# Moving a quarter of one reduction from TensorE to VectorE, and the value masks from VectorE to ScalarE, in a cached-attention decode kernel

## The chip, the cores and the metric

One core of one Trainium2 chip. The metric is the device time of one execution in microseconds (us); lower is better. Several runs are taken and the median is given. One further execution is profiled: its trace gives every instruction's start and duration on each engine, TensorE (PE, with its weight loads as PEld), VectorE (DVE), ScalarE (ACT), GpSimd (POOL) and SyncE (SP, which here only issues DMAs), the semaphores that ended waits, and the DMA packets.

## What is computed

A decode step for 4 batch entries of one token each, model width 512. An adaLN-conditioned attention block with a K and V cache (32 heads of 128, 4096 cached keys), and behind it a gated MLP with a spatial gate:

```python
mod = (_silu(c) @ w_mod).reshape(c.shape[0], 6, 1, -1)
sa, ca, ga, sb, cb, gb = (mod[:, 0], mod[:, 1], mod[:, 2], mod[:, 3], mod[:, 4], mod[:, 5])
h = _layernorm(x) * (1 + ca) + sa
q = (h @ wq).reshape(B, 1, 32, 128).transpose(0, 2, 1, 3)
scores = einsum('bhqd,bhkd->bhqk', q, k_cache) * 128 ** -0.5
o = einsum('bhqk,bhkd->bhqd', softmax(scores), v_cache)
x = x + ga * (o.transpose(0, 2, 1, 3).reshape(B, 1, 4096) @ wo)
h = _layernorm(x) * (1 + cb) + sb
x = x + gb * mixer(h)        # gelu(h @ w_in), halves z1 and layernorm(z2), z1 * (w_sp z2 + b_sp) @ w_out
```

K and V are bf16, 134 MB each. Each cached number is used once.

## The kernel before

**Tiles.** The work on K and V is cut into 32 tiles. Tile i is one batch entry (i mod 4) and one group of four heads (i div 4, eight groups). Its K is 4.19 MB and lies in SBUF as `kt`: 128 partitions by 128 key slots (`NJ`) by 128 numbers (`DH`), partitions 0 to 31 holding the keys of the first head of the group, 32 to 63 those of the second, and so on. V lies the same way as `vt`. There are two buffers for K and two for V.

**Scores of a tile.** With one query there is nothing for TensorE to reuse, so VectorE multiplies K with the query, copied to every partition (`qbc`), in place and in two halves of 64 slots (`mult`, L291). The product then has to be summed over its 128 numbers for each slot. `reduce_d` (L299) does part of that on TensorE: matmuls with the identity add slices of the product in PSUM, 512 columns at a time, 16 matmuls for 64 slots; what is left, 8 partial sums a slot, VectorE adds from PSUM (`sum8`, L318). In tiles 1 to 29, only half of the second 64 slots goes this way (`on_pe` gives 32; 8 matmuls, 16 partial sums a slot), and VectorE sums the other 32 slots straight from SBUF (`sum_rest`, L311).

**Softmax.** `scores` takes the row maximum (L327), spreads it over the 32 partitions of its head by a copy, a 32x32 transpose and a maximum (L329, L331, L333), scales it by -1/sqrt(128) (L334) and has ScalarE take the exponentials head by head into `pbd` (L341), with the row sums `rs`. `norm_r` (L352) puts `rs` into its head's column of `rsb` with a mask; one matmul and a reciprocal (`norm_a`, `norm_b`) give the normaliser for four tiles at once.

**Values.** `pv` (L381) multiplies probabilities with V in 32 matmuls into a PSUM bank (`opss`, two of them); four sets of rows and four column blocks come out, of which each row set has one useful block. `o_pick` (L389, L393) picks them on VectorE with masks `selg`: one product and three multiply-adds of 128x128 f32. `o_cols` (L401) sums the rows that belong together and turns the result with one f32 matmul against `sel4`; `o_scale` (L420, L423) copies it out and normalises it.

**Order.** The order of instructions is written out by hand (a manual schedule), and each engine runs its own in that order. In iteration i: first half product of tile i, softmax of tile i-1, value pick of tile i-3, TensorE sums of the first half, second product, `norm_r` of i-1, `o_scale` of i-3, partial sums of the first half, TensorE sums of the second half, `sum_rest`, then the request for K of tile i+2, which needs the buffer of tile i and so waits for `sum_rest`, then `pv` of i-2 and the request for V of tile i, which waits for `pv` of i-2. All large loads are issued by SP, in this order, on one queue. At iterations 11, 19, 27 and 31 `dealt` regroups finished heads, and `project` multiplies them with `wo`.

**The ends.** Before the first K tile come `wq` and most of `w_mod` (6.8 MB). In iteration 2 the four parts of `wo` and its last rows are loaded; behind the last V come the MLP's weights. Tile 31's V is loaded in five pieces, and the last group of heads (tiles 28 to 31) is handled on its own. Then follow the second layer norm, the MLP and one store.

Of the kernel before, what the change touches and what calls it, by code (L numbers as in the profile page):

```python
# [9 lines left out]
F32 = mybir.dt.float32  # L10
AF = mybir.ActivationFunctionType
ALU = mybir.AluOpType
AX = mybir.AxisListType
PSUM = bass.MemoryType.PSUM

HQ = 4
KC = 64
# [10 lines left out]
def kernel(  # L28
# [16 lines left out]
    nc = tc.nc  # L45
    P = 128
    B, _, D = A_x.shape
    _, H, SK, DH = A_k_cache.shape
# [9 lines left out]
    G = 4  # L58
# [17 lines left out]
    def ps_sm(shape, dtype=F32):  # L76
        return psum.tile(shape, dtype, name="sm", bufs=3)
# [210 lines left out]
    def mult(i, kc):  # L288
        kt = kts[i][:, kc * KC:(kc + 1) * KC, :]
        g, b = divmod(i, B)  # L290
        nc.vector.tensor_tensor(out=kt, in0=kt, in1=bc(qbc[:, g, b, :], KC), op=ALU.mult)  # L291

    def reduce_d(i, kc):
        ns = on_pe(i, kc)
        rd = 512 // ns
        kt = kts[i][:, kc * KC:kc * KC + ns, :]
        red = ps_red().rearrange("p (n r) -> p n r", r=rd)
        for m in range(DH // rd):
            nc.tensor.matmul(  # L299
                red, lhsT=ident_bf, rhs=kt[:, :, m * rd:(m + 1) * rd],  # L300
                start=(m == 0), stop=(m == DH // rd - 1),
            )
        st[i, "red", kc] = red

    def on_pe(i, kc):
        return KC // 2 if kc == 1 and 1 <= i < L - 1 else KC

    def sum_rest(i):
        n0 = KC + on_pe(i, 1)
# [13 lines left out]
    def scores(i):  # L323
        sum8(i, 1)
        S = st.pop((i, "S"))
        mrow = wk.tile([P, 1], F32, name="mrow")
        nc.vector.tensor_reduce(out=mrow, in_=S, axis=AX.X, op=ALU.max)  # L327
        mb = wk.tile([P, R], F32, name="mb")
        nc.vector.tensor_copy(out=mb, in_=mrow.to_broadcast([P, R]))  # L329
        mt = wk.tile([P, R], F32, name="mt")  # L330
        nc.vector.transpose(mt, mb)  # L331
        nM = wk.tile([P, 1], F32, name="nM")
        nc.vector.tensor_reduce(out=nM, in_=mt, axis=AX.X, op=ALU.max)  # L333
        nc.vector.tensor_scalar(  # L334
            out=nM, in0=nM, scalar1=-att_scale, scalar2=None, op0=ALU.mult
        )
        pbd = pbds[i % 3]
        rs = wk.tile([P, 1], F32, name="rs", bufs=3)
        for q in range(HQ):
            r = slice(R * q, R * (q + 1))  # L340
            nc.scalar.activation(  # L341
                out=pbd[r, :, q], in_=S[r, :], func=AF.Exp, bias=nM[r, :],
                scale=att_scale, accum_out=rs[r, :],
            )
        st[i, "rs"] = rs

    def norm_r(i):

        g, b = divmod(i, B)
        if b == 0 or g == NQ - 1:  # L350
            st[g, "rsb"] = wk.tile([P, B, HQ], F32, name="rsb", bufs=2)
        nc.vector.tensor_scalar(  # L352
            out=st[g, "rsb"][:, b, :], in0=mask4, scalar1=st.pop((i, "rs")), scalar2=None, op0=ALU.mult
        )
# [21 lines left out]
    def pv(i):  # L376

        for m in range(NJ // G):
# [4 lines left out]
                start=(m < 4), stop=(m >= NJ // G - 4), tile_position=(0, g),  # L383
            )

    def o_pick(i):
        ops = opss[i % 2]
        osb = wk.tile([P, DH], F32, name="osb")
        nc.vector.tensor_scalar(  # L389
            out=osb, in0=ops[:, 0, :], scalar1=selg[:, 0:1], scalar2=None, op0=ALU.mult  # L390
        )
        for g in range(1, G):
            nc.vector.scalar_tensor_tensor(  # L393
                out=osb, in0=ops[:, g, :], scalar=selg[:, g:g + 1], in1=osb,
                op0=ALU.mult, op1=ALU.add,
            )
        st[i, "osb"] = osb

    def o_cols(i):
        op = ps_sm([P, HQ])  # L400
        nc.tensor.matmul(op, lhsT=st.pop((i, "osb")), rhs=sel4, start=True, stop=True)  # L401
        st[i, "op"] = op
# [9 lines left out]

    def o_scale(i):
        g, b = divmod(i, B)
        op = st.pop((i, "op"))[:, None, :]
        bs = whole(i)
        if g < NQ - 1:
            if b == 0:
                st[g, "o"] = wk.tile([P, B, HQ], F32, name="oU", bufs=2)
            nc.vector.tensor_copy(out=st[g, "o"][:, b:b + 1, :], in_=op)  # L420
            op = st[g, "o"]
        if bs:
            nc.vector.tensor_tensor(  # L423
                out=oTs[:, g * B + bs.start:g * B + bs.stop], in0=op, in1=st.pop((i, "rz")), op=ALU.mult
            )
# [44 lines left out]
    def dealt():  # L470
        if "pp" in st:
            pp, k = st.pop("pp")
            n = SETS[k]
            own = wk.tile([P, n * B, n], F32, name=f"own{n}", bufs=1)
            nc.vector.tensor_tensor(
                out=own, in0=pp.rearrange("p r b h -> p (r b) h"),
                in1=bc(mask8 if n == 2 * HQ else mask4, n * B), op=ALU.mult,
            )
            od = wk.tile([P, n, B], BF16, name="od", bufs=1)
            with nc.allow_low_precision("all but one term of each sum are zero"):  # L480
                nc.vector.tensor_reduce(
                    out=od.rearrange("p r b -> p (r b)"), in_=own, axis=AX.X, op=ALU.add
                )
            st["od"] = od, k
# [60 lines left out]
    for i in range(NT):  # L545
        more = list(QPLAN.get(i, ()))
        mult(i, 0)
        if i >= 1:
            scores(i - 1)
        if i >= 2:  # L550
            norm_b(i - 2)
        add_up()
        rows_up()
        dealt()
        if i >= 3:
            o_pick(i - 3)
        reduce_d(i, 0)
        if i >= 3:
            o_cols(i - 3)
        if more:  # L560
            queries(more.pop(0))
        mult(i, 1)
        if i >= 1:
            norm_r(i - 1)
        if i >= 3:
            o_scale(i - 3)
        sum8(i, 0)
        reduce_d(i, 1)
        sum_rest(i)
        load_k(i + 2)  # L570
        if i >= 1:
            norm_a(i - 1)
        project()
        if i - 3 in ends:
            deal(ends[i - 3])
        while more:
            queries(more.pop(0))
        if i >= 2:
            pv(i - 2)
        if i == 0:  # L580
            load_v(1)
        elif 2 <= i < L:
            load_v(i)
        if i == 2:
            nc.scalar.dma_start(out=sp_t[:, 0:1], in_=B_w_sp[0:1, 0:1])
            nc.scalar.dma_start(out=sp_t[:, 1:2], in_=B_b_sp.rearrange("(a b) -> a b", b=1))
            mps = ps_sm([P, 3 * DJ, B])
            mod_cols(2, 3 * DJ, mps)
            nc.vector.tensor_copy(out=modT, in_=mps)
            pre_cm.__exit__(None, None, None)  # L590
            wts = tl = ctx.enter_context(tc.tile_pool(name="wts", bufs=1))
            wo_sb = wts.tile([P, H - HQ, D], BF16, name="wo_sb")
            wo_last = wts.tile([P, HQ, D], BF16, name="wo_last")
            hl = (H - HQ) * DH
            h0 = 0
            for n in SETS:
                nc.sync.dma_start(
                    out=wo_sb[:, h0:h0 + n, :],
                    in_=A_wo[h0 * DH:(h0 + n) * DH].rearrange("(p r) n -> p r n", p=P),
                )  # L600
                h0 += n
            nc.sync.dma_start(out=wo_last, in_=A_wo[hl:H * DH].rearrange("(q p) n -> p q n", p=P))
        if i == 5:
            sps = ps_sm([P, 2])
            nc.tensor.matmul(sps, lhsT=ones_b, rhs=sp_t, start=True, stop=True)
            nc.vector.tensor_copy(out=spf, in_=sps)
            nc.vector.tensor_copy(out=g8[:, 1, :], in_=spf[:, 0:1].to_broadcast([P, B]))
            cbT = modT[:, 2 * DJ:3 * DJ, :]
            nc.vector.tensor_scalar_add(out=cbT, in0=cbT, scalar1=1.0)
        if i == L - 1:  # L610
            load_v(L)
            win_sb = wts.tile([P, DJ, F], BF16, name="win_sb")
            win = B_w_in.rearrange("(p j) n -> p j n", p=P)
            for ks in KIN:
                nc.sync.dma_start(out=win_sb[:, ks], in_=win[:, ks])
            wout_sb = wts.tile([P, NH, D], BF16, name="wout_sb")
            nc.sync.dma_start(out=wout_sb, in_=B_w_out.rearrange("(j p) n -> p j n", p=P))
            wg_sb = kvp.tile([P, NJ, DH], BF16, name="vt", bufs=2)
            wg_sb = wg_sb.rearrange("p n d -> p (n d)")[:, 0:DJ * D].rearrange("p (k n) -> p k n", k=DJ)
            for ks in KG:  # L620
                nc.sync.dma_start(out=wg_sb[:, ks], in_=wm[:, ks, 5 * D:])
# [186 lines left out]
```

## Time and profile before

| What | Value |
|---|---|
| median of 3 runs | 667.95 us (667.7 to 667.97) |
| profiled execution, device time | 666.9 us |
| its span, first to last instruction | 665.1 us |
| read from HBM | 282.73 MB |
| mean granted TensorE clock | 0.81 of full speed |
| VectorE's longest groups | products L291: 64 of 4.42 us; sums L311: 29 of 4.41 us; partial sums L318: 64 of 0.68 us; picks L393: 93 of 0.35 us |
| TensorE's longest group | L299: 792 matmuls, mean 475 ns |
| ScalarE's longest group | L341: 128 exponentials, 577 ns each, and 128 reads of the sum, 251 ns each |

The busy share of an engine is over the whole span. A row of a group gives line, engine, operation, tiles and shapes, count, busy time, the mean time of one, and the idle time before them with what ended it. A line of the timeline gives start, duration, engine, line, operation and shapes; a bracket at its end holds idle time before it and what ended that.

### The profile page before, as it was taken

The page shows a single profiled execution, that of the slowest core. Times are in us where ns is not written, and L with a number is a line of the kernel's source. Part 1 is how long each engine was busy: PE and PEld are TensorE (multiplying, and loading weights), DVE is VectorE, ACT ScalarE, POOL GpSimd, SP SyncE. Part 2 cuts the span into 40 slices and gives each one's busy share as a digit, 9 for nine tenths or more (in the row PEclk, how much of TensorE's full clock was granted, in tenths as well). Part 3 has the DMA queues.
Part 4 walks back from the last instruction along what each step waited for, and adds up shares of the span by engine and source line. Part 5 has one row for each costly group of instructions (what it writes and reads, how often), then busy time and mean ns, then how long its engine had stood idle before and what let it go on. Part 6 is the DMA issues. An engine that isn't in the chain of part 4 may idle for free.

```text
span 665.1 us, 6076 instructions
## 1 busy us (share of the span) xinstructions
PE 343.7 (52%) x2442; PEld 151.9 (23%) x2442; DVE 544.9 (82%) x618; ACT 85.1 (13%) x278; POOL 3.8 (1%) x17
## 2 busy tenths in 40 slices
PE   1194655545345545634564456455434456654676
PEld 0131322212122222211221122222212122321235
DVE  3488797888888998888798889889888888988833
ACT  1021111111011111100111110111111011111112
POOL 1000000000000000000000000000000000000000
PEclk9997899667888877788877778987778888777875
DMA  8999999999999999999999999999999999999996
GB/s 363 456 413 437 437 413 439 438 425 430 438 438 419 437 437 433 424 438 437 425 428 442 437 418 437 440 434 423 436 439 427 432 433 441 426 433 426 441 414 246
DMA packets 13535, 283.12 MB, mean 426 GB/s; under 512 B 1340, under 2 KB 3268, under 8 KB 4420
## 3 DMA queue, kind: packets, MB, share of 16 engines
q1 hardware_dynamic: 13488, 282.73, 99.0%
q8 instruction: 19, 0.31, 0.2%
q14 instruction: 8, 0.07, 0.0%
q10 hardware_dynamic: 20, 0.01, 0.0%
HBM read 282.73 MB, written 0.00 MB: 425 GB/s over the span
## 4 chain that ended last, share of the span: by engine, by line
DMA 55%; DVE 41%; PE 2%; issue 1%; SPq 0%; ACT 0%; DVEq 0%
DMA kt<-in_A_k_cache_dram 50%; DVE kt L291 22%; DVE S L311 10%; DMA vt<-in_A_v_cache_dram 3%; DVE S L318 3%; DMA wout_sb<-in_B_w_out_dram 2%; DVE osb L393 2%; PE red L299 1%; DVE mrow L327 1%; DVE osb L389 1%; DVE mt L331 1%; DVE nM L333 0%; DVE mb L329 0%; DVE nM L334 0%; DVE rsb L352 0%
## 5 line engine op out<-in xcount | busy, mean ns | idle before, releaser
L299 PE MATMUL red<-kt,ident_bf 128*128 128x512 bf16 x792 | 245.3, 475 | 292.3 <-DVE kt L291 292.3
L291 DVE TENSOR_TENSOR kt<-kt,qbc 128x8192 bf16<-128x8192 bf16 x64 | 282.8, 4420 | 69.4 <-DMA kt<-in_A_k_cache_dram 68.5
L299 PEld LDWEIGHTS <-ident_bf 128*128 128x128 bf16 x792 | 94.9, 120 | 434.5 <-issue 285.6
L341 ACT ACTIVATE pbd<-S,nM 32x128 bf16<-32x128 f32 x128 | 73.9, 577 | 508.0 <-DVE nM L334 465.7
L311 DVE TENSOR_REDUCE S<-kt 128x32 f32<-128x4096 bf16 x29 | 127.8, 4408 | 0.0
L381 PE MATMUL ops<-vt,pbd 128*16 128x512 bf16 x992 | 62.8, 389 | 1.8 <-DMA vt<-in_A_v_cache_dram 1.8
L318 DVE TENSOR_REDUCE S<-red 128x64 f32<-128x512 f32 x64 | 43.7, 683 | 6.7 <-PE red L299 6.7
L393 DVE SCALAR_TENSOR_TENSOR osb<-ops,selg,osb 128x128 f32<-128x128 f32 x93 | 32.6, 351 | 3.3
L341 ACT ACTIVATION_READ_ACCUMULATOR pbd<-S,nM 32x1 f32 x128 | 32.1, 251 | 0.0
L381 PEld LDWEIGHTS <-pbd 128*16 128x16 bf16 x992 | 23.2, 90 | 31.4 <-issue 9.2
L389 DVE TENSOR_SCALAR osb<-ops,selg 128x128 f32<-128x128 f32 x31 | 10.1, 324 | 5.7 <-PE ops L381 5.7
L401 PEld LDWEIGHTS sm<-sel,osb 128*128 128x128 f32 x62 | 11.7, 194 | 6.8 <-issue 2.2
L281 ACT CAST qbc<-qps 128x512 bf16<-128x512 f32 x8 | 4.7, 586 | 42.4 <-PE qps L277 42.4
L401 PE MATMUL sm<-sel,osb 128*128 128x4 f32 x62 | 9.1, 218 | 1.9 <-DVE osb L393 1.7
L327 DVE TENSOR_REDUCE mrow<-S 128x1 f32<-128x128 f32 x32 | 9.2, 286 | 1.1
L277 PE MATMUL qps<-wq_sb,hTb 128*32 128x512 bf16 x128 | 9.2, 412 | 1.6 <-DVE hTb L265 0.9
L331 DVE STREAM_TRANSPOSE mt<-mb 128x32 f32<-128x32 f32 x32 | 6.8, 212 | 1.1
L352 DVE TENSOR_SCALAR rsb<-mask,rs 128x4 f32<-128x4 f32 x32 | 7.2, 224 | 0.4 <-ACT pbd L341 0.4
L245 PE MATMUL sm<-cT,wm_sb 128*128 128x4 bf16 x80 | 3.0, 173 | 8.3 <-DMA wm_sb<-in_w_mod_dram 8.3
L259 DVE SCALAR_TENSOR_TENSOR hs<-sm,xn 128x16 f32<-128x16 f32 x1 | 0.2, 173 | 8.6 <-PE sm L245 8.6
L333 DVE TENSOR_REDUCE nM<-mt 128x1 f32<-128x32 f32 x32 | 5.9, 186 | 1.1
L329 DVE COPY mb<-mrow 128x32 f32<-128x32 f32 x32 | 5.8, 182 | 1.1
(137 smaller groups left out, 99.9 us busy)
## 6 DMA issues: line engine op xcount, KB each, us to landing
kt<-in_A_k_cache_dram SPq DMA_DIRECT2D x31, 4096.0 KB, 21.4
vt<-in_A_v_cache_dram SPq DMA_DIRECT2D x31, 4096.0 KB, 30.7
wq_sb<-in_A_wq_dram SPq DMA_DIRECT2D x1, 4096.0 KB, 12.2
kt<-in_A_k_cache_dram SPq DMA_DIRECT2D x2, 2048.0 KB, 16.5
wo_sb<-in_A_wo_dram SPq DMA_DIRECT2D x3, 1024.0 KB, 24.9
kt<-in_A_v_cache_dram SPq DMA_DIRECT2D x3, 1024.0 KB, 26.9
wm_sb<-in_w_mod_dram SPq DMA_DIRECT2D x1, 2560.0 KB
win_sb<-in_B_w_in_dram SPq DMA_DIRECT2D x2, 896.0 KB, 23.7
```

Source lines behind the costliest of these rows:

```text
L277: nc.tensor.matmul(qp[R * q:R * (q + 1)], lhsT=hTb[:, k, b, :], rhs=wq_v[:, k, gs, q, :], start=(k == 0), stop=(k == DJ - 1), tile_positio ...
L291: nc.vector.tensor_tensor(out=kt, in0=kt, in1=bc(qbc[:, g, b, :], KC), op=ALU.mult)
L299: nc.tensor.matmul(red, lhsT=ident_bf, rhs=kt[:, :, m * rd:(m + 1) * rd], start=(m == 0), stop=(m == DH // rd - 1),)
L311: nc.vector.tensor_reduce(out=st[i, "S"][:, n0:NJ], in_=kts[i][:, n0:NJ, :], axis=AX.X, op=ALU.add)
L318: nc.vector.tensor_reduce(out=st[i, "S"][:, kc * KC:kc * KC + on_pe(i, kc)], in_=st.pop((i, "red", kc)), axis=AX.X, op=ALU.add,)
L327: nc.vector.tensor_reduce(out=mrow, in_=S, axis=AX.X, op=ALU.max)
L331: nc.vector.transpose(mt, mb)
L341: nc.scalar.activation(out=pbd[r, :, q], in_=S[r, :], func=AF.Exp, bias=nM[r, :], scale=att_scale, accum_out=rs[r, :],)
L381: nc.tensor.matmul(opss[i % 2][g:g + G * HQ], lhsT=pbds[i % 3][:, n, :], rhs=vts[i][:, n, :], start=(m < 4), stop=(m >= NJ // G - 4), tile ...
L389: nc.vector.tensor_scalar(out=osb, in0=ops[:, 0, :], scalar1=selg[:, 0:1], scalar2=None, op0=ALU.mult)
L393: nc.vector.scalar_tensor_tensor(out=osb, in0=ops[:, g, :], scalar=selg[:, g:g + 1], in1=osb, op0=ALU.mult, op1=ALU.add,)
L401: nc.tensor.matmul(op, lhsT=st.pop((i, "osb")), rhs=sel4, start=True, stop=True)
```

## The change

Four edits, in tiles 1 to 29 or 0 to 27:

- `on_pe` gives 16 instead of 32 slots of the second half to TensorE in tiles 1 to 29: 4 matmuls instead of 8, 32 partial sums a slot (512 columns as before), and `sum_rest` has 48 slots, 6144 elements a partition, instead of 32.
- The row maximum: the scale is put into the spreading copy, and the maximum behind the transpose becomes a minimum; the separate scaling of `nM` goes.
- `norm_r` runs on ScalarE for the first seven head groups (tiles 0 to 27).
- The value pick for tiles 0 to 27: ScalarE masks the four blocks (`o_mask`, issued right behind the first product of the tile three later and ahead of the exponentials on ScalarE) into a new tile `osg`; VectorE sums the four with one reduction; `o_cols` is a transpose of 128x128 f32 by the identity, and `o_scale` sums its 128 columns to 4 with a reduction in place of the copy. `dealt` borrows `osg` for its product and comes behind the pick. Tiles 28 to 31 keep the old way.

```diff
     def on_pe(i, kc):
-        return KC // 2 if kc == 1 and 1 <= i < L - 1 else KC
+        return KC // 4 if kc == 1 and 1 <= i < L - 1 else KC
...
-        nc.vector.tensor_copy(out=mb, in_=mrow.to_broadcast([P, R]))
+        nc.vector.tensor_scalar(
+            out=mb, in0=mrow.to_broadcast([P, R]), scalar1=-att_scale, scalar2=None, op0=ALU.mult
+        )
...
-        nc.vector.tensor_reduce(out=nM, in_=mt, axis=AX.X, op=ALU.max)
-        nc.vector.tensor_scalar(
-            out=nM, in0=nM, scalar1=-att_scale, scalar2=None, op0=ALU.mult
-        )
+        nc.vector.tensor_reduce(out=nM, in_=mt, axis=AX.X, op=ALU.min)
...
+        if g < NQ - 1:
+            nc.scalar.activation(
+                out=st[g, "rsb"][:, b, :], in_=mask4, func=AF.Copy, scale=st.pop((i, "rs"))
+            )
+            return
...
+    def o_mask(i):
+        osg = wk.tile([P, G, DH], F32, name="osg", bufs=1)
+        for g in range(G):
+            nc.scalar.activation(
+                out=osg[:, g, :], in_=opss[i % 2][:, g, :], func=AF.Copy, scale=selg[:, g:g + 1]
+            )
+        st[i, "osg"] = osg
+
     def o_pick(i):
...
+        if i // B < NQ - 1:
+            nc.vector.tensor_reduce(
+                out=osb, in_=st.pop((i, "osg")).rearrange("p g d -> p d g"), axis=AX.X, op=ALU.add
+            )
+            st[i, "osb"] = osb
+            return
...
     def o_cols(i):
+        if i // B < NQ - 1:
+            op = ps_sm([P, P])
+            nc.tensor.transpose(op, st.pop((i, "osb")), ident_f)
+            st[i, "op"] = op
+            return
...
-            nc.vector.tensor_copy(out=st[g, "o"][:, b:b + 1, :], in_=op)
+            nc.vector.tensor_reduce(
+                out=st[g, "o"][:, b, :], in_=op.rearrange("p (c q) -> p q c", q=HQ), axis=AX.X, op=ALU.add
+            )
...
         mult(i, 0)
+        if 3 <= i and (i - 3) // B < NQ - 1:
+            o_mask(i - 3)
...
-        dealt()
         if i >= 3:
             o_pick(i - 3)
+        dealt()
         reduce_d(i, 0)
```

More of the change, by code (lines that the diff above doesn't have):

```diff
@@ L384, in pv @@
             )
+    def o_mask(i):
[5 more added lines that the diff above has]
+        st[i, "osg"] = osg
     def o_pick(i):
         ops = opss[i % 2]
-        osb = wk.tile([P, DH], F32, name="osb")
+        osb = wk.tile([P, DH], F32, name="osb", bufs=1)
+        if i // B < NQ - 1:
[4 more added lines that the diff above has]
+            return
         nc.vector.tensor_scalar(
@@ L414, in o_scale @@
         g, b = divmod(i, B)
-        op = st.pop((i, "op"))[:, None, :]
+        op = st.pop((i, "op"))
         bs = whole(i)
@@ L419, in o_scale @@
                 st[g, "o"] = wk.tile([P, B, HQ], F32, name="oU", bufs=2)
-            nc.vector.tensor_copy(out=st[g, "o"][:, b:b + 1, :], in_=op)
+            nc.vector.tensor_reduce(
+                out=st[g, "o"][:, b, :], in_=op.rearrange("p (c q) -> p q c", q=HQ), axis=AX.X, op=ALU.add
+            )
             op = st[g, "o"]
+        else:
+            op = op[:, None, :]
         if bs:
@@ L473, in dealt @@
             n = SETS[k]
-            own = wk.tile([P, n * B, n], F32, name=f"own{n}", bufs=1)
+            if n == 2 * HQ:
+                own = wk.tile([P, G, DH], F32, name="osg", bufs=1)
+                own = own.rearrange("p g d -> p (g d)")[:, 0:n * B * n].rearrange("p (a h) -> p a h", h=n)
+            else:
+                own = wk.tile([P, n * B, n], F32, name=f"own{n}", bufs=1)
             nc.vector.tensor_tensor(
```

## The prediction

> **What bounds the kernel now.** I read the busy shares and DMA rows of the page first, then the windows, then VectorE's waits and the order of one tile on VectorE.
>
> ```profile
> span 665.1 us, 6076 instructions
> PE 343.7 (52%) x2442; PEld 151.9 (23%) x2442; DVE 544.9 (82%) x618; ACT 85.1 (13%) x278; POOL 3.8 (1%) x17
> ...
> DMA  8999999999999999999999999999999999999996
> GB/s 363 456 413 437 437 413 439 438 425 430 438 438 419 437 437 433 424 438 437 425 428 442 437 418 437 440 434 423 436 439 427 432 433 441 426 433 426 441 414 246
> ...
> kt<-in_A_k_cache_dram SPq DMA_DIRECT2D x31, 4096.0 KB, 21.4
> vt<-in_A_v_cache_dram SPq DMA_DIRECT2D x31, 4096.0 KB, 30.7
> ```
>
> The DMA engines are full from the second slice to the last but one. The last two rows show why: a K load of 4096 KB (4.19 MB) needs 9.7 us at 432 GB/s, but lands 21.4 us after it is asked for, so about 11.7 us of other transfers are still ahead of it in SP's queue. The queue never runs dry. The windows show the rate without the noise of short slices:
>
> ```profile
> core 0: us, PE busy (x) PEld busy (x) DVE busy (x) ACT busy (x) POOL busy (x), PEclk, DMA share, GB/s
> ...
> 120.00:220.00 100.00, 48.79 (x295) 19.98 (x295) 87.84 (x89) 11.57 (x40) 0.00 (x0) 0.77 1.00 432
> ...
> 520.00:620.00 100.00, 55.13 (x349) 24.77 (x350) 87.60 (x89) 11.58 (x40) 0.00 (x0) 0.81 1.00 432
> ...
> 655.00:665.00 10.00, 5.41 (x113) 4.53 (x113) 3.58 (x19) 3.77 (x8) 1.08 (x5) 0.50 0.38 137
> ```
>
> 432 GB/s early and late, with VectorE busy 88 us in 100 and TensorE 49 to 55. So the kernel streams 282.7 MB at a fixed rate, and only the last 5 us (the output work behind the last weights) are not transfer time. VectorE keeps pace and then waits for each K tile; the waits and one tile (number 15) show by how much:
>
> ```profile
> DVE kt L291 <- DMA kt<-in_A_k_cache_dram: 68.5, 30, 5.6
> ```
>
> ```profile
> 311.59 4.42 DVE L291 TENSOR_TENSOR kt<-kt,qbc 128x8192 bf16<-128x8192 bf16 x1 [2.01 <-DMA kt<-in_A_k_cache_dram]
> ...
> 317.65 0.15 DVE L334 TENSOR_SCALAR nM<-nM 128x1 f32<-128x1 f32 x1
> 317.73 0.34 DVE L389 TENSOR_SCALAR osb<-ops,selg 128x128 f32<-128x128 f32 x1
> 318.10 1.12 DVE L393 SCALAR_TENSOR_TENSOR osb<-ops,selg,osb 128x128 f32<-128x128 f32 x3
> 319.14 4.42 DVE L291 TENSOR_TENSOR kt<-kt,qbc 128x8192 bf16<-128x8192 bf16 x1
> 323.48 0.22 DVE L352 TENSOR_SCALAR rsb<-mask,rs 128x4 f32<-128x4 f32 x1
> 323.61 0.16 DVE L420 COPY oU<-sm 128x4 f32<-128x4 f32 x1
> 323.68 0.68 DVE L318 TENSOR_REDUCE S<-red 128x64 f32<-128x512 f32 x1
> 324.28 4.41 DVE L311 TENSOR_REDUCE S<-kt 128x32 f32<-128x4096 bf16 x1
> 332.03 4.43 DVE L291 TENSOR_TENSOR kt<-kt,qbc 128x8192 bf16<-128x8192 bf16 x1 [3.35 <-DMA kt<-in_A_k_cache_dram]
> ```
>
> The bracket at the end of a line is idle time and what ended it. A tile is 17.1 us of VectorE (311.59 to 328.69). Over tiles 7 to 30 the work is 17.1 to 17.9 us, K tiles land about every 19.4 us, and the wait is 1.44 to 3.35 us, mean 2.1. That is the cover for whatever the change adds. The chain that ended last lists VectorE lines for 41% of the span only because each K load is asked for when a tile is done; those requests come 11.7 us before they are needed.
>
> **The change, part by part (VectorE, per tile).**
>
> Sums of key slots. L311 takes 4.41 us for 4096 elements, and the reductions of 128 and 32 elements (L327 0.286, L333 0.186 us) give 1.04 ns an element and 0.15 us fixed, which fits L311 too. 6144 elements: 6.54 us, +2.13. The other reduction (L318) still reads 512 elements from PSUM and stays. The Trainium skill (VectorE: DVE Perf Modes, Rules for kernel authors) says that a reduction only runs at the one-fold rate, is VectorE's slowest operation and should be restructured away from a hot path; L311 agrees (4096 elements in the time of an 8192-element product). By that rule alone the change moves work the wrong way and would cost 29 x 2.13 = 62 us; by the waits it costs nothing as long as it stays under them.
>
> Picking the value rows. The four instructions L389 and L393 take 317.73 to 319.14, 1.41 us. In their place stands one reduction of 512 f32 elements read with a stride. Before has no such row; the nearest:
>
> ```profile
> L145 DVE TENSOR_REDUCE sel<-ident_f 128x32 f32<-128x128 f32 x1 | 0.4, 376 | 0.3 <-POOL ident_f masks.py:199 0.3
> ...
> L159 DVE TENSOR_REDUCE sel<-ident_f 128x4 f32<-128x128 f32 x1 | 0.4, 370 | 0.0
> ```
>
> Low end 0.68 us (L318, 512 elements in order); high end 1.50 (four times the strided L145). I take 1.05: L145 less the fixed 0.15 is 1.74 ns an element, times 512, since L145 is the nearest strided form. So -0.36 (-0.73 to +0.09).
>
> Row maximum. The scaling L334 goes, 0.08 us from start to start (0.15 whole); the copy L329 becomes a multiply (0.18 to 0.22, as L352). -0.04 (-0.15 to 0).
>
> rsb and oU. L352 goes to ScalarE and the copy L420 becomes a reduction of 128 strided elements: together 0.20 us before (323.48 to 323.68); now 0.37 (L159 has this form), of which the next instruction overlaps 0.09. +0.1 (0 to +0.2).
>
> Sum: +2.13 - 0.36 - 0.04 + 0.1 = **+1.8 us a tile, between +1.25 and +2.4**. Against a wait of 2.1 it disappears: VectorE's busy time rises to about 593 us (544.9, + 61.8 for the long sums, - 9.6 for the picks, - 3.6 for the row maxima, - 0.3 for rsb and oU, by whole durations), its wait for K falls from 68.5 to under 20 us. Tiles with 1.44 us of wait push 0.4 us into the next tile, which takes it up.
>
> TensorE. 29 x 4 matmuls of 475 ns leave (-55 us of 245 on that line); the f32 matmul pair L401 (0.41 us of loads, 0.28 of matmul) becomes a transpose (0.38, as L774). TensorE waits for VectorE anyway (292.3 us at L299). New wait: oU needs that transpose, which stands behind 16 matmuls of L299; these took up to 6.1 us after the first product, at half clock throughout 6.9, plus about 0.5, while VectorE comes to oU 7.2 us after it. Cost 0 to 0.25; I take 0. Behind oU stand L318, the long sum and the next K request.
>
> ScalarE. Four masks of 128x128 from PSUM a tile, between 0.20 (small activations) and 0.59 us (the 128x512 CAST of L281): 1.2 us at 0.29 each. They wait for the value matmuls of tile i-3, which end before the next tile's first product begins (the 1.9 us of L381 from 325.43, next tile 332.03), in front of the exponentials, which come over 5 us into the tile. ScalarE is idle 17 us of each tile just there. Cost 0; if that cover went, the exponentials and then the value matmuls, and with them V's request, would be late by at most 2.4 us, against 11.7 us of queue.
>
> SP's queue. No DMA is added or moved. K requests come up to 1.8 us later. The tightest is tile 4's: it is asked for at 74.75, when the transfer in front of it lands at 78.41. Tile 1's growth fits in the 2.65 us that tile 2 waited for its K; tile 2 ends 1.9 us later (no value rows to pick yet), so 76.6: 1.8 us ahead. At the start of the kernel a request at 0.73 moved data within the window 1 to 2 us, so a lead of about 1 us is enough. Cost 0; at most 1 if the queue ran dry.
>
> The end. Tiles 30 and 31 keep their old sums. The last weights land at 661.2 and the end follows from them. Cost 0.
>
> Sum against the profiled execution: 665.1 + 0, and 1.8 around the span, 666.9. That execution is 1.05 us under the median 667.95, so on the median's scale: 667.95, **forecast 667.9**.
>
> **Rivals.**
>
> 1. Slower: VectorE becomes the bound. The point is a growth over the mean wait of 2.1 us a tile. Stepping tile by tile through the shown work and K landings, +2.2 leaves a lag of about 1 us at tile 31, +2.4 one of 6, +2.6 one of 11. The end has 2.4 us of slack in series: TensorE idles 1.8 us (641.6 to 643.42) before the last full V tile; the LN sums end 0.3 us before the last V piece; the output product waits 0.3 us for its weights. So +2.4 gives about 671.4, +2.6 about 677; 0.2% is crossed near +2.3. For it: the strided sum is unpriced and its high end lies there. Against: it would have to cost four L145s, at a fixed part paid four times over.
>
> 2. The queue runs dry at tile 4: at most 1 us, 668.9, still within 0.2%. For it: the margin halves from 3.7 to 1.8 us. Against: the 1 us lead above.
>
> 3. Faster. The clock granted to TensorE is 0.50 in the last 10 us; with less TensorE work earlier it might be 1.0. But the output product starts only when its weights are there (659.83), so only its 0.91 us and the last transpose's 0.38 halve: -0.6, 667.3, not 0.2%. More would need a DMA rate over 432 GB/s (433.4 gives -1.3 us, 666.6); the windows vary by 1 GB/s whatever the engines do, and no part of the change touches transfers.
>
> **How the numbers follow.** 0.2%, 1.3 us, is about what a measurement of this kernel can tell from no change (its runs spread over 0.27 us). No change 0.80 (the forecast and rival 2, which has 0.10 of it); slower, rival 1, 0.13; faster, rival 3 with a higher rate, 0.07. Range: from 666.9 (rival 3's clock and the runs' spread) to 670.0 (rival 1 at about +2.35); that leaves out some 0.15.
>
> **What would show it.** Right: L311's successor near 6.5 us; the strided sum near 1 us; the wait of the first product for K still there in nearly every tile; DMA 9s and 432 GB/s in the same windows; last weights landing near 661. Wrong: K loads landing less than 12 us after their request, or first products with no wait, tile after tile, and the wait at osb on ScalarE or at oU on TensorE.

## The result and the profile after

The changed kernel takes 667.94 us (median of 14 runs, 667.64 to 669.06) against 667.08 us (14 runs, 666.82 to 668.02) of the kernel before on the same chips: ratio 1.0015, interval 1.0008 to 1.0022. The forecast was 667.9 with no change. That the absolute number came out is luck: the kernel before measures 667.1 in the larger set of runs and not 667.95, and against it the change costs 0.9 us. That is within the 0.2% I called "no change", but it is beyond its interval, so there is a loss to be found. The profiled execution took 667.65 us with a span of 665.9.

The page of the kernel after, busy shares and transfers:

```profile
span 665.9 us, 5788 instructions
PE 318.6 (48%) x2298; PEld 135.8 (20%) x2298; DVE 591.5 (89%) x474; ACT 125.4 (19%) x418; POOL 3.8 (1%) x17
...
DMA  8999999999999999999999999999999999999996
GB/s 366 452 419 431 383 423 442 425 436 437 431 426 437 438 428 429 435 439 426 429 437 435 431 431 432 437 429 432 435 435 428 435 432 435 433 430 426 438 417 268
```

VectorE is at 89% as forecast and the DMA digits are the same. One slice stands out: the fifth (66.6 to 83.2 us) moved 383 GB/s where it was 437 before. 54 GB/s over 16.6 us is 0.9 MB, about 2 us of transfer. One tile of VectorE in steady state, tile 14, and VectorE's wait for K over the whole span:

```profile
294.18 4.42 DVE L291 TENSOR_TENSOR kt<-kt,qbc 128x8192 bf16<-128x8192 bf16 x1 [0.66 <-DMA kt<-in_A_k_cache_dram]
...
299.56 0.18 DVE L329 TENSOR_SCALAR mb<-mrow 128x32 f32<-128x32 f32 x1
...
300.12 1.01 DVE L402 TENSOR_REDUCE osb<-osg 128x128 f32<-128x512 f32 x1
301.06 4.40 DVE L291 TENSOR_TENSOR kt<-kt,qbc 128x8192 bf16<-128x8192 bf16 x1
305.39 0.27 DVE L443 TENSOR_REDUCE oU<-sm 128x4 f32<-128x128 f32 x1
...
306.39 6.54 DVE L311 TENSOR_REDUCE S<-kt 128x48 f32<-128x6144 bf16 x1
313.58 4.43 DVE L291 TENSOR_TENSOR kt<-kt,qbc 128x8192 bf16<-128x8192 bf16 x1 [0.65 <-DMA kt<-in_A_k_cache_dram]
```

```profile
DVE kt L291 <- DMA kt<-in_A_k_cache_dram: 29.0, 26, 5.6
```

The tile is 18.75 us long (17.31 before) and VectorE still waits for the next K, 0.65 us. So in the steady state the cover held. The place of the loss is the early slice. There stands tile 2's long sum, for which the request for tile 4's K waits, before first:

```profile
70.28 4.41 DVE L311 TENSOR_REDUCE S<-kt 128x32 f32<-128x4096 bf16 x1
```

```profile
70.30 6.54 DVE L311 TENSOR_REDUCE S<-kt 128x48 f32<-128x6144 bf16 x1
```

SP's requests in both kernels around 75 us (K of tile 4, then V of tile 2), before first:

```profile
74.75 0.33 SPq L107 DMA_DIRECT2D kt<-in_A_k_cache_dram  x1
75.18 0.38 SPq L107 DMA_DIRECT2D vt<-in_A_v_cache_dram  x1
```

```profile
76.91 0.33 SPq L107 DMA_DIRECT2D kt<-in_A_k_cache_dram  x1
77.33 0.38 SPq L107 DMA_DIRECT2D vt<-in_A_v_cache_dram  x1
```

And the windows there, before first. The last two columns are DMA share and GB/s; both count a packet whole in the window in which it starts, so that a share can exceed 1:

```profile
76.00:78.00 2.00, 0.83 (x25) 0.74 (x23) 0.21 (x1) 0.00 (x0) 0.00 (x0) 1.00 1.05 426
```

```profile
76.00:78.00 2.00, 0.00 (x0) 0.00 (x0) 0.96 (x2) 0.00 (x0) 0.00 (x0) 1.00 0.60 180
```

Tile 4's K is asked for 2.16 us later, and the DMA share falls from 1.05 to 0.60. The packet records of the trace say it more exactly: in the kernel before there are at least 16 packets in flight, as many as there are DMA engines, all the way from 5 to 655 us (the shortfall at 76 us is 0.05 us of all engines). In the kernel after there is one gap in that stretch: it opens at 76.3 us, and on average each engine is without a packet for 1.3 us; from 76 to 78 us the engines are 43% busy. There is no other gap in 650 us. The first 16 packets behind the gap also take 1.85 us on average, where a packet otherwise takes 1.21. Later K tiles land 0.9 to 2.0 us later than before, and the last weights land at 662.02 instead of 661.16; from there to the end it is about 3.9 us in both. Why less than the gap is left at the end in these two executions is not shown; single tiles come up to 1 us earlier or later from one kernel to the next.

### The profile page after: what moved, and what is told of

It reads as the page before. It is cut to its first block, busy times and chain, and to the rows that moved or that the text cites. A ratio compares the mean times of both kernels' runs of the same rounds, so it can differ in the third digit from the quotient of the medians.

```text
span 665.9 us, 5788 instructions
## 1 busy us (share of the span) xinstructions
PE 318.6 (48%) x2298; PEld 135.8 (20%) x2298; DVE 591.5 (89%) x474; ACT 125.4 (19%) x418; POOL 3.8 (1%) x17
## 4 chain that ended last, share of the span: by engine, by line
DMA 51%; DVE 45%; PE 3%; issue 1%; SPq 1%; ACT 0%; DVEq 0%
DMA kt<-in_A_k_cache_dram 46%; DVE kt L291 22%; DVE S L311 15%; DMA kt<-in_A_v_cache_dram 4%; DVE S L318 3%; DVE osb L402 2%; PE red L299 1%; DVE mrow L327 1%; DVE mt L333 1%; DVE mb L329 0%; DVE nM L335 0%; DVE oU L443 0%; SPq L107 0%; PE ops L385 0%; PE sm L195 0%
## 5 line engine op out<-in xcount | busy, mean ns | idle before, releaser
L299 PE MATMUL red<-kt,ident_bf 128*128 128x512 bf16 x676 | 221.5, 494 | 318.1 <-DVE kt L291 318.1
L311 DVE TENSOR_REDUCE S<-kt 128x48 f32<-128x6144 bf16 x29 | 189.6, 6537 | 0.0
L299 PEld LDWEIGHTS <-ident_bf 128*128 128x128 bf16 x676 | 81.5, 121 | 453.3 <-issue 272.5
L393 ACT ACTIVATE osg<-ops,selg 128x128 f32<-128x128 f32 x112 | 32.0, 368 | 164.0 <-PE ops L385 164.0
L402 DVE TENSOR_REDUCE osb<-osg 128x128 f32<-128x512 f32 x28 | 28.0, 1000 | 0.0
L352 ACT ACTIVATE rsb<-mask,rs 128x4 f32<-128x4 f32 x28 | 8.3, 297 | 1.0
L443 DVE TENSOR_REDUCE oU<-sm 128x4 f32<-128x128 f32 x28 | 7.7, 276 | 0.0
L420 PE MATMUL sm<-ident_f,osb 128*128 128x128 f32 x28 | 7.6, 273 | 0.0
L329 DVE TENSOR_SCALAR mb<-mrow 128x32 f32<-128x32 f32 x32 | 5.8, 182 | 1.1
```

The lines of the kernel that those rows point to most:

```text
L299: nc.tensor.matmul(red, lhsT=ident_bf, rhs=kt[:, :, m * rd:(m + 1) * rd], start=(m == 0), stop=(m == DH // rd - 1),)
L311: nc.vector.tensor_reduce(out=st[i, "S"][:, n0:NJ], in_=kts[i][:, n0:NJ, :], axis=AX.X, op=ALU.add)
L352: nc.scalar.activation(out=st[g, "rsb"][:, b, :], in_=mask4, func=AF.Copy, scale=st.pop((i, "rs")))
L393: nc.scalar.activation(out=osg[:, g, :], in_=opss[i % 2][:, g, :], func=AF.Copy, scale=selg[:, g:g + 1])
L402: nc.vector.tensor_reduce(out=osb, in_=st.pop((i, "osg")).rearrange("p g d -> p d g"), axis=AX.X, op=ALU.add)
```

## Experiments

Theory A: the whole loss is that gap, made by tile 2 alone. Theory B: it is spread over the tiles (VectorE at 89%, K requests 2 us later everywhere, ScalarE reading PSUM). Ratios are to runs of the kernel before on the same chip.

### Tile 2 of the changed kernel gets its old share back

```diff
-        return KC // 4 if kc == 1 and 1 <= i < L - 1 else KC
+        return (KC // 2 if i == 2 else KC // 4) if kc == 1 and 1 <= i < L - 1 else KC
```

> The changed kernel, but tile 2 alone keeps the old share (32 slots of its second half on TensorE, 32 on VectorE); tiles 1 and 3 to 29 keep the new one. Theory A (the lost time is one gap in the transfer queue, 1.27 us at 76.3 us, because tile 2's longer sum asks for tile 4's K at 76.9 instead of 74.75): the request comes back to about 74.6, no DMA engine idles between 5 and 655 us, and the time is that of the kernel before, ratio 1.000 (0.9995 to 1.0005). Theory B (the loss is spread over the tiles: VectorE busy 89% instead of 82%, K requests 2 us later in every tile, ScalarE's reads of PSUM): one tile in 29 changes almost nothing, ratio 1.0012 to 1.0015.

666.77 us, ratio 0.9997 (0.9988 to 1.0005). The request went out at 75.26, the gap shrank to under 0.1 us, and the loss is gone with 28 tiles still on the new share and waits for K of mostly 0.5 to 0.8 us, as in the changed kernel. Theory B in every form that lives in the other tiles is excluded at the size of the loss.

### Tile 2 of the kernel before gets the new share

```diff
-        return KC // 2 if kc == 1 and 1 <= i < L - 1 else KC
+        return (KC // 4 if i == 2 else KC // 2) if kc == 1 and 1 <= i < L - 1 else KC
```

> The kernel before, with one tile changed: tile 2 sums 48 of its slots on VectorE instead of 32. Theory A: tile 4's K is asked for 2.1 us later, at about 76.9, the DMA engines idle about 1.2 us there, and the whole kernel is 0.8 to 1.3 us longer, ratio 1.0012 to 1.002. Theory B: one tile's 2.1 us of VectorE is hidden by the wait for K like any other, ratio 1.000.

668.23 us, ratio 1.0019 (1.0010 to 1.0028); gap 1.3 us. Tile 2's longer sum alone, put into the kernel before, brings all of the loss. It is 1.2 us here and 0.9 in the changed kernel; measured against the previous experiment instead (ratios 1.0015 and 0.9997), the changed kernel's gap costs about 1.2 us too (an estimate). The window of this kernel:

```profile
76.00:78.00 2.00, 0.00 (x0) 0.00 (x0) 1.06 (x2) 0.00 (x0) 0.00 (x0) 1.00 0.29 98
```

### All new sums, but V asked for ahead of K in iteration 2

```diff
-        load_k(i + 2)
+        if i != 2:
+            load_k(i + 2)
...
         elif 2 <= i < L:
             load_v(i)
+            if i == 2:
+                load_k(i + 2)
```

> The changed kernel with all its sums, but in iteration 2 alone V of tile 2 is asked for ahead of K of tile 4. V's buffer comes free when TensorE has finished the value matmuls of tile 0, at about 74 us, before the long sum ends. Theory A: the queue has V's 9.7 us when the engines run out of tile 3's K at 76.3, the gap is gone although VectorE's work is unchanged, ratio 1.000 (0.9993 to 1.0005); tile 4 starts 1 to 2 us later than in the changed kernel and the later tiles 1 us earlier. Theory B: nothing else has changed, ratio 1.0012 to 1.0015.

666.60 us, ratio 0.9993 (0.9984 to 1.0002). SP's requests and the window:

```profile
74.59 0.33 SPq L107 DMA_DIRECT2D vt<-in_A_v_cache_dram  x1
77.17 0.33 SPq L107 DMA_DIRECT2D kt<-in_A_k_cache_dram  x1
```

```profile
76.00:78.00 2.00, 0.23 (x7) 0.14 (x5) 1.26 (x2) 0.00 (x0) 0.00 (x0) 1.00 1.07 426
```

K is asked for even later than in the changed kernel, VectorE's work is the same, and the loss is gone, because V stands in the queue. So it is not the late K that costs, nor the longer sum: it is the empty queue.

### All edits but the sums

```diff
-        return KC // 4 if kc == 1 and 1 <= i < L - 1 else KC
+        return KC // 2 if kc == 1 and 1 <= i < L - 1 else KC
```

> The changed kernel with the old share of sums in all tiles (32 slots on VectorE), all other edits kept: the masks and rsb on ScalarE, the strided sum, the transpose, the minimum. Theory A: VectorE's tile is about 0.5 us shorter than before, tile 4's K is asked for no later than in the kernel before, no gap: ratio 1.000 (0.9993 to 1.0004); the wait for K grows to about 80 us and buys nothing. Theory B in the form that ScalarE's reads and the transpose cost: ratio above 1.0005.

666.84 us, ratio 0.9998 (0.9989 to 1.0006). The masks and rsb on ScalarE, the strided sum and the transpose cost nothing, and the 0.7 us of VectorE that they free in each tile buy nothing: its waits for K grow to 1.9 to 3.9 us a tile from tile 6 on.

### A longer delay in tile 2

```diff
-        return KC // 2 if kc == 1 and 1 <= i < L - 1 else KC
+        return (KC // 8 if i == 2 else KC // 2) if kc == 1 and 1 <= i < L - 1 else KC
```

> The kernel before, with tile 2 alone summing 56 of its slots on VectorE instead of 32 (7168 elements, 7.6 us, +3.2). Theory A: the gap grows with every microsecond by which the request for tile 4's K is late, so with the request at about 78.0 the engines idle about 2.4 us and the kernel is 2.0 to 2.5 us longer, ratio 1.003 to 1.0038. A rival, that the gap is a fixed price of a dry queue whatever its length: about 1.2 us again, ratio 1.0019.

669.35 us, ratio 1.0038 (1.0026 to 1.0050). The request goes out at 77.98:

```profile
70.30 7.61 DVE L311 TENSOR_REDUCE S<-kt 128x56 f32<-128x7168 bf16 x1
```

```profile
76.00:78.00 2.00, 0.00 (x0) 0.00 (x0) 2.00 (x2) 0.00 (x0) 0.00 (x0) 1.00 0.12 49
```

The gap grows to 2.2 us and the time by 2.3. From 32 to 48 to 56 slots, the request goes from 74.75 to 77.01 to 77.98, the gap from 0.05 to 1.3 to 2.2, the time from 0 to 1.2 to 2.3: the price is the length of the gap, not a fixed one. It also gives the margin of the kernel before. With 48 and 56 slots the request comes 1.53 and 0.41 us before the transfer in front lands; a straight line through the two gaps ends at about 3.2 us. The kernel before, at 3.7, had about half a microsecond to spare (an estimate).

### VectorE's share raised until it is the bound

```diff
-        return KC // 4 if kc == 1 and 1 <= i < L - 1 else KC
+        return (KC // 2 if i <= 2 else KC // 8) if kc == 1 and 1 <= i < L - 1 else KC
```

> The changed kernel with 56 slots on VectorE in tiles 3 to 29 and the old share in tiles 1 and 2 (no early gap). It tests the point from which VectorE is the bound: a tile's VectorE work, 18.7 us on average in the changed kernel, grows by 1.07 to about 19.8 against 19.35 us between K landings, so VectorE falls behind by about 0.4 us a tile, 10 to 12 us by tile 31. Less the 2.4 us of slack at the end, the kernel should be 6 to 10 us longer, ratio 1.009 to 1.015, the waits for K gone from the middle of the run. If VectorE's share did not matter there (transfers hide it), ratio 1.000.

672.16 us (four runs, 671.11 to 674.26), ratio 1.0083 (1.0066 to 1.0099): 5.1 us at the medians, a little under the 6 to 10 expected. Waits for K before (68.5 us in 30), and in this kernel:

```profile
DVE kt L291 <- DMA kt<-in_A_k_cache_dram: 11.1, 3, 5.6
```

The three left are in tiles 0, 2 and 3; from tile 4 on VectorE never waits. A tile takes 19.8 us (118.11 to 613.54 for 25 tiles), as expected, and tile 30 begins 9.9 us later than before. Tile 31 begins at 625.94 instead of 618.21, a lag of 7.7 us and not 10 to 12: I had not counted that tile 30, which has no long sum, gives back 2.1 us, of which 1.5 are a wait for K that is gone. 7.7 less the 2.4 us of slack at the end would be 5.3, but the trace does not show it to come about in this way. The last weights land 5.3 us later than before (666.50 against 661.16), and the end follows 3.8 us behind them (4.0 before): the lag reaches the end through the transfers. They slow down late in the run:

```profile
220.00:320.00 100.00, 43.66 (x273) 16.99 (x273) 99.10 (x62) 18.76 (x65) 0.00 (x0) 0.74 1.00 433
...
420.00:520.00 100.00, 42.67 (x264) 16.79 (x263) 99.14 (x65) 19.04 (x66) 0.00 (x0) 0.72 1.00 421
```

VectorE is busy 99% here and the rate is 421 GB/s from 420 us on, where it is 431 to 434 in the kernels before and after. The first engines are without a packet at 416 us, when the requests go out 7.4 us later than in the kernel before (415.28 against 407.87). That is the steady state's real margin; I had taken 11.7. Up to 655 us the engines are without a packet for 1.5 us; slower packets (see the last section) account for some 3 us more, so that the two make up most of the 5.1.

### The longer sums alone, without the edits that relieve VectorE

The kernel before, with the new share in tiles 1 and 3 to 29 and the old one in tile 2:

```diff
-        return KC // 2 if kc == 1 and 1 <= i < L - 1 else KC
+        return (KC // 2 if i == 2 else KC // 4) if kc == 1 and 1 <= i < L - 1 else KC
```

> The kernel before with 48 slots on VectorE in tiles 1 and 3 to 29 and the old share in tile 2: the longer sums alone, without any of the edits that take work off VectorE. Growth +2.13 us a tile against a mean wait of 2.1: the stepping gives a lag of 0 to 1 us at tile 31, under the 2.4 us of slack, ratio 1.000 (0.9995 to 1.0007), nearly no wait for K left. If the edits that take work off VectorE were needed to pay for the sums, ratio above 1.001.

666.84 us, ratio 0.9998 (0.9989 to 1.0006). The waits for K are 10.7 us in all, most tiles have none, and tile 31 begins at 617.86, no later than before. At about +2.1 us a tile VectorE is just even with the transfers, and that is still free. So the other edits were not needed to pay for the sums.

### The kernel before with V ahead of K in iteration 2

The edit is that of the third experiment, in the kernel before.

> The kernel before, with V of tile 2 asked for ahead of K of tile 4 in iteration 2, nothing else. Theory A: before has next to no gap there (0.05 us), so there is nothing to win: ratio 1.000 (0.9994 to 1.0004). If the order of these two loads is worth something by itself, as the 0.9993 of the same order in the changed kernel may suggest, ratio 0.9993 or lower.

667.05 us, ratio 1.0003 (0.9995 to 1.0012). No gap to close, nothing won: the 0.9993 of the third experiment is no gain of the order.

No version here beats the kernel before beyond its interval. That fits the cause: with the gap closed, the first, third, fourth, seventh and eighth kernel all have full engines from 5 to 655 us, but for less than 0.1 us.

## Why the prediction was wrong where it was

**The bound.** Right. Transfers set the time, at 431 to 434 GB/s in every window from 120 to 620 us of both kernels; 2 us more of VectorE in nearly every tile is free (the sums alone, ratio 0.9998), and 0.7 us less is worth nothing.

**VectorE's growth.** Forecast +1.8 us a tile (1.25 to 2.4), measured +1.5 (tiles 3 to 29, from the first product to the next wait). The rows of the kernel after:

```profile
L311 DVE TENSOR_REDUCE S<-kt 128x48 f32<-128x6144 bf16 x29 | 189.6, 6537 | 0.0
...
L393 ACT ACTIVATE osg<-ops,selg 128x128 f32<-128x128 f32 x112 | 32.0, 368 | 164.0 <-PE ops L385 164.0
...
L402 DVE TENSOR_REDUCE osb<-osg 128x128 f32<-128x512 f32 x28 | 28.0, 1000 | 0.0
...
L443 DVE TENSOR_REDUCE oU<-sm 128x4 f32<-128x128 f32 x28 | 7.7, 276 | 0.0
```

The long sum is 6.537 us (6.54 forecast). The strided sum is 1.00 us (1.05): scaling L145's rate an element came nearer than the bounds, 0.68 and 1.50. The sum to `oU` is 0.276, not 0.37; L159 was a poor model although its form is the same, and what made it slow at 3 us into the kernel is open. With rsb gone to ScalarE, VectorE spends 0.20 us there, as before. The scaled copy is 0.18, not 0.22, and the row maximum saves 0.20 us, more than the 0.15 I had as its bound: from the start of the last of its instructions to the next one it is 0.10 us now (300.02 to 300.12 in tile 14) and was 0.30 with the scaling between (317.43 to 317.73 in tile 15). I had counted the scaling's 0.08 us, but not that it started 0.22 us behind the maximum, where the next instruction now starts after 0.10. Idle time before `osb` and `oU` is 0.0: the waits for ScalarE and for the transpose that could have come did not. The Trainium skill's rule (VectorE: DVE Perf Modes, Rules for kernel authors) that a reduction on a hot path be restructured has the price on its side: 6144 elements take 6.54 us, where a product of 8192 takes 4.42. But VectorE's path is not the hot one here.

**ScalarE.** A mask is 0.368 us, not 0.29; 1.5 us a tile, all in idle time.

**TensorE.** Forecast -55 us on L299, measured -24 (245.3 to 221.5). I priced the 116 matmuls that left with the mean of the group, 475 ns, as if they ran one behind the other; but they overlap (792 of 475 ns would be 376 us, and the line is busy for 245), and those that left came in quick bursts (8 in 1.89 us at a granted clock of 1.00, 0.24 each). 116 x 0.24 is 27. It changed nothing.

**SP's queue: the step that failed.** "The tightest is tile 4's [...] 76.6: 1.8 us ahead. [...] a lead of about 1 us is enough. Cost 0; at most 1 if the queue ran dry." This term of the sum, put at 0, is the loss: 0.9 us here, 1.2 where tile 2's longer sum stands alone. The place was right, the time of the request nearly so (76.91, not 76.6), and so was the lead: the first packet of that K starts at 77.87, 0.96 us after its request. Wrong was what the request was held against. I took the landing of the transfer in front, 78.41, for the moment when the queue is empty. But the landing is when the last engine is done. The packet records show the last packets of tile 3's K starting up to 76.84 and ending between 76.3 and 78.06, since each takes 1.2 us and the engines do not run in step; the landing follows 0.4 us after the last end. The first engine is empty at 76.3, 2.2 us ahead of the landing (78.48 in this kernel). With the lead, a request has to come about 3 us before the landing of what is in front, and there were 1.6. By the same working the kernel before, 3.7 us ahead, had a little to spare. Its 0.05 us of gap is another thing: a single engine, whose first packet of tile 4's K starts only at 77.57, 2.8 us after the request; why is open. The Trainium skill (DMA: Bandwidth & Descriptors, Anatomy of one DMA) puts a fixed cost of about 2 us on a DMA of the GpSimd path, most of it between the last byte and the semaphore; these DMAs are SP's, and here I measure 0.4 us there and the rest as engines out of step, but a sum that had taken 2 us off the landing would have found the gap, though for another reason.

**The rivals.** Rival 2 was the case, and the halved margin that I named for it was its cause; I gave it 0.10 of the chance and priced it at most 1 us; the gap was 1.3 us and the loss 0.9 to 1.2. Of the signs I had listed, only the rate shows it, and only in the first window (20 to 120 us: 420 GB/s, before 429). Rival 1's stepping held where I pushed the kernel there: at +2.47 us a tile the lag at tile 31 was 7.7 us, between the 6 and 11 given for +2.4 and +2.6. Its 2.4 us of slack at the end was not put to the test, since the 5.1 us came through the transfers. Rival 3 did not come: the last windows' clock stayed at 0.50.

## What to carry to other kernels

A queue of transfers begins to run empty when its first engine does, not when the last transfer lands: hold a later request against the landing in front less the time by which the engines are out of step (here about 2 us), less the lead of a request (here 1 us). When the stream is the bound, look for the one request with the least queue ahead of it (here at a change of phase, tile 2, and not in the equal tiles behind it); delays elsewhere are free up to their own margin (here about 7 us), there every microsecond counts once. The cheap cure is not a faster engine but another transfer that is already free to go, put ahead in the queue.

## What was not expected of the hardware

- The granted clock over the span was 0.81 before and 0.76 after, but 0.78 also with all edits but the sums, which leaves L299 all its 792 matmuls; what lowered it is open. The mean matmul of L299 went from 475 to 494 ns mostly because quick ones left. The 464 of the first halves of tiles 1 to 29, the same in both kernels, went from 522 to 532 ns and from 160.3 to 164.4 us of busy time: some 4 of the 28 us that left were paid back.
- Packets behind a late request are slow, so that the transfers lose time even while the engines count as busy: in the kernel with 56 slots the DMA share stays at 1.00 from 420 to 520 us while the rate is 421 GB/s. In the packet records of 100 to 620 us, a 32 KB packet takes 1.214 us on average in the kernels before and after, and 1.222 there, with the slowest hundredth over 1.5 us instead of 1.21; over the stretch that is some 3 us, more than the engines idled. Three quarters of the slow ones (over 1.3 us) start within 4 us of a request for K or V, but only a fifth of all packets. Why they are slow is open.
